# Attention with squared relu and a mixture of adapters: a written order table, and a last batch in two parts with q and k turned by DMA

## The chip, the cores and the metric

The kernel runs on one core of a Trainium2 chip, which has TensorE (PE), VectorE (DVE), ScalarE (ACT), GpSimd (POOL) and SyncE (SP). The metric is the device time of one execution in microseconds (us), taken as the median of a few runs; lower is better. One further execution was taken by the hardware profiler.

## The reference

Eight batches of twelve heads, 448 positions, 64 channels a head. The attention has no softmax: the scores are cut at zero and squared. Its output rows then go through a mixture of eight rank-16 adapters, of which each row uses two.

```python
scores = scale * np.matmul(q, k.transpose(0, 1, 3, 2))          # 8 x 12 x 448 x 448
attn = np.maximum(scores, 0.0) ** 2 / S
x = np.matmul(attn, v)                                          # -> (3584, 768)
logits = x @ w_gate
topk = np.argpartition(-logits, K, axis=1)[:, :K]               # K = 2 of 8
w = np.exp(sel) / (np.exp(sel).sum() + 1e-09)                   # over the two
out = x + sum(w[e] * ((x @ A[e]) @ B[e]) for e in topk)
```

## The kernel before

*Tiling.* A batch is worked on in three quads of four heads; a quad is held as two groups of 64 partitions and two slots. For each of the 24 pairs of batch and quad POOL loads q, k and v (L306), casting them to bf16. PE transposes q and k, 56 small transposes each (L430, `tp`), and DVE copies the result out of PSUM as qT (L444; L452 for the first ones). Then, for each of seven key tiles of 64 keys, PE forms the scores of the quad against all 448 queries (L571, `qk`; four 64x64 matmuls), ACT or DVE applies the scaled relu from PSUM into bf16 (L591 or L593; 128x896 elements), and DVE squares two or three such results at once (L609, `sq`). PE multiplies by v and sums over the seven key tiles in PSUM (L635, `pv`), and ACT or DVE copies the finished 448 columns to xt (L664), which holds the attention output transposed, in bf16. There are 168 key tiles (`n` from 0 to 167).

*The adapters.* The 3584 output rows make 28 tiles of 128, numbered 0 to 27; tile t needs columns 128t to 128t+127 of xt, so tiles 24 to 27 need the last batch, whose columns are 3136 to 3583. Tiles are taken in groups of three, at the end of two, one and one (`gl`). PE multiplies a tile by A and the gate weights at once (L681, six matmuls); the gate chain on DVE with one sigmoid on ACT (L702 to L725) picks two experts and scales; PE transposes the result (L742, `zt`) and it is copied to zT (L751). Each tile's output is made in two halves of 384 columns. PE brings x back by three identity matmuls (L796) and adds the fp32 product with B (L801), 20 PE instructions for a whole tile, and ACT or DVE copies the half out (L836). For tiles 15 to 23 SP has turned x by DMA instead (L767, `xb`, six transposes of 128x384 for a group), and DVE adds it to the product (L831). SP stores a tile from one of four output buffers (`osb`) in two transfers (L852); tiles 24 and 26 are stored by ACT, and tile 27 half by SP and half by ACT.

*The order of the work.* `build` makes a list of operations with their dependencies, ranks and durations. `schedule` is a planner: it plays the list through with a model of engines, PSUM banks and buffers, and each free engine takes the ready operation of lowest rank. The two tables `RANKS` and `ENGINES` nudge single operations. The program is emitted in the order of its start times, each engine running its part in order. PSUM banks and, where an operation can run on ACT or DVE, the engine come from the planner too. The code has a path for turning q and k by DMA (`turn_qk`, `qk_turned`), used from batch `bx` on; with `bx=8` no batch takes it. On that path SP turns q once and k twice, the second time shifted by 64 columns, after DVE has copied k's first 64 columns behind its end (`dup`). The queries then stand in the order 1, 3, 5, 0, 2, 4, 6 of blocks of 64.

The scores go from a pool of four buffers (`a1`, from relu to square) to one of seven (`a2`, from square to the product with v), and the first product of a quad also waits for a square six key tiles ahead (`late`).

Of the kernel before, what the change touches and what calls it, by code (L numbers as in the profile page):

```python
# [14 lines left out]
J = 7  # L15
# [10 lines left out]
STORES = {24: "ACT", 26: "ACT"}  # L26
# [3 lines left out]
PARTS = {b: ((0, S),) for b in range(NB)}  # L30

def parts(*cuts):
    x = [0, *cuts, S]
    return tuple(zip(x, x[1:]))


C = dict(
    tp_=2.3287, qk_=-3.679, sq_=3.7975, pv_=3.3372, xt_=-1.2131, gate_=-0.65203, id_=-0.78412,  # L40
    out_=-0.80943, zt_=6.6019, a12=(4, 7), late=6, merge_x=0, id2=2.6063, ocap=3, tboth=1, sqs=(2, 2, 3), xback=(15, 23), xblat=1.4, xbdur=1.35, bx=8, xlag=6, xh=2, apart=3, gl=(2, 1), tqk=-25.0, tqlat=2.0,
    slack=-0.19633, switch=5.8334, third=4.0894, dve_relu=0.28627, relu_until=400, qk=-2.3217, sq=10,
    pv=1.0506, xt=8.4423, tp=-9.2867, tpe=4.3867, gate_mm=-4.8593, gate=-1.4524, zt=0.2432, zte=2.902,
    id=15.183, out=3.032, pace=6.5353,
)
POOLS = dict(qT=5, a1=C["a12"][0], a2=C["a12"][1], zp=2, zT=3, osb=4, w=3, q=5, k=5, v=8, xb=3)

RANKS = {  # L50
    0: 5, 84: 115, 85: 162, 86: 87, 132: 10, 141: 53, 148: -11, 150: 39, 155: -32, 156: -8, 157: 13, 158:
    -9, 160: -12, 163: -20, 166: -25, 170: -15, 179: -51, 185: -11, 191: -5, 192: 35, 200: 50, 210: 36,
    214: 47, 216: 67, 219: -52, 221: -10, 224: -18, 229: -25, 230: -23, 234: 23, 237: 31, 256: 58, 257:
    61, 276: 60, 290: -45, 292: 8, 310: -28, 314: 54, 318: 3, 321: 23, 332: 49, 342: 72, 350: 58, 355:
    -35, 360: -83, 363: 29, 374: -15, 375: -17, 377: -7, 379: 29, 394: 4, 409: -1, 424: 24, 427: 74, 446:
    -9, 451: -35, 456: 7, 459: 102, 463: -61, 471: -10, 490: 4, 500: -12, 503: -13, 511: 52, 517: 30,
    519: -28, 531: -4, 542: 6, 543: 16, 550: 63, 558: 45, 562: 70, 564: 80, 567: -7, 572: -39, 574: -59,
# [5 lines left out]
    1065: -149,  # L63
}
ENGINES = {
    140: "ACT", 178: "ACT", 233: "ACT", 265: "ACT", 286: "ACT", 298: "ACT", 568: "ACT", 634: "DVE", 852:
    "ACT", 866: "ACT", 881: "ACT",
}

# [16 lines left out]
class Op:  # L86
    def __init__(self, engs, dur, fn, deps=(), after=None, mode=None, kind="", take=(), give=(),
# [12 lines left out]
        for d in self.deps + [after] * (after is not None):  # L100
            d.users.append(self)


class Dma:


    def __init__(self):
# [926 lines left out]
```

## Time and profile before

| what | us |
|---|---|
| median of 3 runs (182.50 to 183.17) | 183.02 |
| span of the profiled execution | 181.7 |
| first relu on ACT starts | 6.7 |
| last relu on ACT ends | 160.2 |
| last PE matmul ends | 176.8 |
| last copy out of PSUM ends | 177.4 |

Durations that matter, from the table of groups (mean of one; neighbours on ACT, and a little on DVE, overlap, so that in a row they cost less):

| line, engine | what | count | mean ns |
|---|---|---|---|
| L591 ACT | relu 128x896 | 155 | 961 |
| L593 DVE | relu 128x896 | 13 | 1088 |
| L609 DVE | square 128x1792 / 128x2688 | 48 / 24 | 1085 / 1550 |
| L444 DVE | qT copy 128x1792 | 21 | 1084 |
| L664 ACT / DVE | xt copy 128x448 | 28 / 20 | 576 / 618 |
| L836 ACT / DVE | osb copy 128x384 | 25 / 13 | 532 / 556 |
| L831 DVE | osb addition 128x384 | 18 | 550 |
| L571, L635 PE | scores, product with v, 64x448 | 672 each | 367, 350 |
| L801 PE | fp32 product with B, two records each | 112 | 515 |

The shares of the page give busy time over the span. A busy PE is not a PE at its peak: matmuls are pipelined, and the records of neighbours overlap. In the chain of waits, where matmuls follow each other, four of 64x448 take 0.19 us and 56 transposes 0.48 us.

### The profile page before, as it was taken

The page shows a single profiled execution, that of the slowest core. Times are in us where ns is not written, and L with a number is a line of the kernel's source. Part 1 is how long each engine was busy: PE and PEld are TensorE (multiplying, and loading weights), DVE is VectorE, ACT ScalarE, POOL GpSimd, SP SyncE. Part 2 cuts the span into 40 slices and gives each one's busy share as a digit, 9 for nine tenths or more (in the row PEclk, how much of TensorE's full clock was granted, in tenths as well). Part 3 has the DMA queues.
Part 4 walks back from the last instruction along what each step waited for, and adds up shares of the span by engine and source line. Part 5 has one row for each costly group of instructions (what it writes and reads, how often), then busy time and mean ns, then how long its engine had stood idle before and what let it go on. Part 6 is the DMA issues. An engine that isn't in the chain of part 4 may idle for free.

```text
span 181.7 us, 7410 instructions
## 1 busy us (share of the span) xinstructions
PE 164.6 (91%) x3198; PEld 96.1 (53%) x3198; DVE 164.7 (91%) x257; ACT 155.5 (86%) x229; POOL 89.8 (49%) x155
## 2 busy tenths in 40 slices
PE   7868698897999998999999999999999999999990
PEld 2433266574465565554755556565654456446640
DVE  1589999999999997999999999999999999998860
ACT  3679999999999997999999999999999999951200
POOL 7999968898786678924975769200000000000000
PEclk9978999999999999999999999999999999999996
DMA  5999999999999999994999999993538264457676
GB/s 92 119 166 151 170 230 136 166 170 185 174 184 186 203 222 194 190 233 108 201 190 257 246 214 199 223 143 78 110 73 203 49 150 112 116 138 208 174 195 156
DMA packets 34450, 30.49 MB, mean 168 GB/s; under 512 B 11952, under 2 KB 30896, under 8 KB 34416
## 3 DMA queue, kind: packets, MB, share of 16 engines
q0 software_dynamic: 22000, 17.03, 64.3%
q1 hardware_dynamic: 11792, 11.90, 24.8%
q10 hardware_dynamic: 624, 1.08, 2.3%
q8 instruction: 25, 0.41, 0.9%
q14 instruction: 9, 0.07, 0.2%
HBM read 33.84 MB, written 11.01 MB: 247 GB/s over the span
## 4 chain that ended last, share of the span: by engine, by line
PE 58%; ACT 17%; DVE 14%; issue 4%; DMA 2%; POOL 2%; ACTq 0%; DVEq 0%; POOLq 0%
PE ps L801 19%; PE ps L571 14%; ACT a L591 14%; PE ps L635 11%; DVE a L609 7%; PE ps L681 4%; PE ps L796 4%; PE ps L430 3%; DMA k<-in_k_dram 2%; DVE qT L444 2%; ACT xt L664 2%; PE ps L382 2%; DVE xt L664 2%; POOL q L306 1%; DVE a L593 1%
## 5 line engine op out<-in xcount | busy, mean ns | idle before, releaser
L591 ACT ACTIVATE a<-ps 128x896 bf16<-128x896 f32 x155 | 133.9, 961 | 2.8 <-PE ps L571 2.5
L609 DVE TENSOR_TENSOR a<-a 128x1792 bf16<-128x1792 bf16 (+1 forms) x72 | 88.5, 1240 | 1.4 <-ACT a L591 1.3
L571 PE MATMUL ps<-qT 64*64 64x448 bf16 x672 | 58.6, 367 | 6.6 <-ACT a L591 4.3
L801 PE MATMUL ps<-B,zT 128*128 128x384 f32 x112 | 47.5, 515 | 0.0
L635 PE MATMUL ps<-a,v 64*64 64x448 bf16 x672 | 43.0, 350 | 1.7 <-ACT a L591 1.6
L571 PEld LDWEIGHTS <-qT 64*64 64x64 bf16 x672 | 22.5, 105 | 35.1 <-issue 27.5
L306 POOL DMA_DIRECT2D q<-in_q_dram x48 | 29.3, 629 | 13.4 <-PE ps L571 6.0
L306 POOL DMA_DIRECT2D v<-in_v_dram x48 | 29.2, 630 | 7.9 <-DMA k<-in_k_dram 4.4
L306 POOL DMA_DIRECT2D k<-in_k_dram x46 | 28.1, 632 | 4.0 <-PE ps L571 2.1
L635 PEld LDWEIGHTS <-v 64*64 64x64 bf16 x672 | 21.7, 106 | 12.0 <-issue 4.8
L444 DVE COPY qT<-ps 128x1792 bf16<-128x1792 bf16 x21 | 22.8, 1084 | 0.2
L801 PEld LDWEIGHTS ps<-B,zT 128*128 128x128 f32 x112 | 17.4, 191 | 4.5 <-DVE osb L831 0.9
L664 ACT CAST xt<-ps 128x448 bf16<-128x448 f32 x28 | 15.2, 576 | 3.6 <-PE ps L635 3.6
L593 DVE TENSOR_SCALAR a<-ps 128x896 bf16<-128x896 f32 x13 | 14.1, 1088 | 0.5 <-PE ps L571 0.4
L681 PE MATMUL ps<-awg,xt 128*128 128x136 bf16 x168 | 12.8, 223 | 1.0 <-issue 0.9
L836 ACT COPY osb<-ps 128x384 f32<-128x384 f32 x25 | 12.8, 532 | 0.6 <-PE ps L801 0.2
L681 PEld LDWEIGHTS <-xt 128*128 128x128 bf16 x168 | 10.4, 98 | 5.5 <-issue 5.0
L796 PE MATMUL ps<-identb,xt 128*128 128x128 bf16 x114 | 12.7, 220 | 0.2
L796 PEld LDWEIGHTS <-xt 128*128 128x128 bf16 x114 | 7.8, 97 | 9.7 <-issue 8.1
L664 DVE CAST xt<-ps 128x448 bf16<-128x448 f32 x20 | 12.2, 618 | 0.7 <-PE ps L635 0.5
L430 PEld LDWEIGHTS <-q 64*64 64x64 bf16 x672 | 10.3, 110 | 4.1 <-DMA q<-in_q_dram 1.2
L430 PE MATMUL ps<-identb,q 64*64 64x64 bf16 x672 | 10.5, 195 | 0.7 <-DMA q<-in_q_dram 0.3
(47 smaller groups left out, 99.0 us busy)
## 6 DMA issues: line engine op xcount, KB each, us to landing
out_dram<-osb SPq DMA_DIRECT2D x50, 192.0 KB, 3.9
q<-in_q_dram POOLq DMA_DIRECT2D x48, 112.0 KB, 4.8
v<-in_v_dram POOLq DMA_DIRECT2D x48, 112.0 KB, 5.1
k<-in_k_dram POOLq DMA_DIRECT2D x46, 112.0 KB, 4.9
out_dram<-osb ACTq DMA_DIRECT2D x4, 192.0 KB, 2.6
B<-in_moe_B_dram POOLq DMA_DIRECT2D x1, 384.0 KB, 6.9
xb<-xt SPq DMA_TRANSPOSE x18, 2.7
a_raw<-in_moe_A_dram POOLq DMA_DIRECT2D x1, 192.0 KB, 6.5
```

Source lines behind the costliest of these rows:

```text
L306: nc.gpsimd.dma_start(out=t[g * PH : g * PH + PH], in_=k.qkv[w][b, g, :, 2 * q : 2 * q + 2, :])
L430: nc.tensor.transpose(k.ps_b[sl * PH : sl * PH + PH, o.banks[g], (w * J + j) * PH : (w * J + j) * PH + PH], source(w, j)[r, sl], k.identb[ ...
L444: nc.vector.tensor_copy(t.rearrange("p g w x -> p g (w x)"), k.ps_b[:, m.banks[0] : m.banks[0] + 2, : 2 * S])
L571: nc.tensor.matmul(out=bank(o, sl)[g * PH : g * PH + PH, at : at + w], lhsT=t[r, g, 1, j * PH : j * PH + PH], rhs=t[r, g, 0, x0:x1], start ...
L591: nc.scalar.activation(out, flat(qk_ops[n], w), ACTF.Relu, scale=k.relu_scale)
L593: nc.vector.tensor_scalar(out, flat(qk_ops[n], w), k.relu_scale, 0.0, op0=ALU.mult, op1=ALU.max)
L609: nc.vector.tensor_mul(a2, T["a1", g0], T["a1", g0])
L635: nc.tensor.matmul(out=bank(head, g)[sl * PH : sl * PH + PH, :w], lhsT=vn[r, sl, j * PH : j * PH + PH], rhs=T["a2", g0][r, i, sl * w : sl ...
L664: evac(w, lambda cp, g=g: cp(k.xt[:, g * QUADS + q, b * S + x0 : b * S + x1], bank(src, g)[:, :w]), deps=[pv_ops[n]], free=[(src, g)], ran ...
L681: nc.tensor.matmul(out=bank(zops[0])[:, t * ZW : t * ZW + ZW], lhsT=k.xt[:, do, 128 * tiles[t] : 128 * tiles[t] + 128], rhs=k.awg[:, do, : ...
L796: nc.tensor.matmul(out=out(h)[:, x * 128 : x * 128 + 128], lhsT=k.xt[:, 3 * h + x, c0 : c0 + 128], rhs=k.identb, start=(x == 0), stop=Fals ...
L801: nc.tensor.matmul(out=out(h)[:, :W], lhsT=T["zT", g0][:, zi], rhs=k.B[:, h * W : h * W + W], start=xb is not None, stop=True, skip_group_ ...
```

## The change

The planner, its ranks and its costs are gone. `ORDER` is a table of words, one for each operation, in the order in which the program is emitted. A word names the operation (`f4` and the like: loads and small things of the start), behind `@` its PSUM bank, behind `:` the engine, A for ACT and D for DVE. `ordered` puts the list of `build` into this order.

The last batch takes the path with q and k turned by DMA (`bx=7`), and its queries are done in two parts: first 320 for all three quads, one key tile at a time, then the other 128, with the scores of four and then three key tiles in one pair of PSUM banks and one relu of 1024 or 768 elements. The key tiles are then 174 numbers, 147 to 167 for the first part and 168 to 173 for the second. The last groups of tiles have three and one (`gl`). There is one pool `a` of eleven buffers; the square is written in place, and the wait on a square six tiles ahead is gone. Other new arguments (`xi`, `om`, `z64`) are off.

In the table `qt63` to `qt71` are the nine DMA transposes of q and k, `xb` those of x, `st` the stores, `b` an output half of PE and `o` its copy (number 2t or 2t+1 for tile t), `z`, `zt` and the `g` words the gate chain.

```diff
-PARTS = {b: ((0, S),) for b in range(NB)}
+PARTS = {b: ((0, S, 1),) for b in range(NB)}
+PARTS.update({7: ((0, 320, 1), (320, 448, 4))})
...
-    out_=-0.80943, zt_=6.6019, a12=(4, 7), late=6, merge_x=0, id2=2.6063, ocap=3, tboth=1, sqs=(2, 2, 3), xback=(15, 23), xblat=1.4, xbdur=1.35, bx=8, xlag=6, xh=2, apart=3, gl=(2, 1), tqk=-25.0, tqlat=2.0,
+C = dict(late=6, xi=(), om=(), merge_x=0, sqs=(2, 2, 3), xback=(15, 23), xblat=1.4, xbdur=1.35, bx=7, xlag=6, xh=2, apart=3, gl=(3, 1), tqlat=2.0)
+GROUP = 2688
...
-POOLS = dict(qT=5, a1=C["a12"][0], a2=C["a12"][1], zp=2, zT=3, osb=4, w=3, q=5, k=5, v=8, xb=3)
+POOLS = dict(qT=5, a=11, zp=2, zT=3, osb=4, w=3, q=5, k=5, v=8, xb=3)
...
+ORDER = """
+f4 f3 f0 f1 f6 f2 f5 f11 f7 f8 f9 f10 f84@0 f85@2 f12 f88 f90 f89 f13 qk0@4 qk1@6 relu0:D qk2@0 relu1:A f14
+f87@2 f91 tp2@4 relu2:A qk3@6 te2 f15 qk4@2 relu3:A relu4:D qk5@0 tp3 relu5:A f17 qk6@6 te3 relu6:A sq0 qk7@2
+qk8@0 qk9@4 relu7:A tp4@6 f16 relu8:D relu9:A qk10@2 te4 qk11@0 relu10:A qk12@4 relu11:D tp5 f18 relu12:A qk13@2
...
+gt12 pv105@2 relu122:D pv106 gsg12 pv107 o21:A qk123@4 pv108 f79 pv109 relu123:A gw12 st20 pv110 gzp12 pv111
+qk124@0 x223:D qk125@6 relu124:A pv112@4 pv113 relu125:D qt65 zt12@3 zt13 zt14 x222:A pv114 qk126@0 zT12:A sq121
+pv115 pv116 relu126:A pv117 f72 qk127@6 pv118 qk128@2 sq123 relu127:A xb90 b24@0 relu128:A b28@1 x236:D xb93
+o24:A sq119 x237:A qk129@6 tp38@2 f75 tp39 relu129:A qk130@4 xb91 te38 b25@0 relu130:A o28:D qk131@6 o25:A
+tp40@2 xb94 tp41 relu131:A sq128 qk132@4 pv119@0 f82 pv120 pv121 relu132:A te40 qk133@6 st24 pv122 pv123
+relu133:A pv124 f78 qk134@4 sq130 qk135@2 pv125 relu134:A qt68 b26@6 x250:A b29@7 dup23 x251:D relu135:A xb92
+sq126 o26:A qk136@4 qk137@0 qk138@2 relu136:A z15@6 o29:D z16 relu137:D relu138:A st28 f81 qk139@4 z17 relu139:A
+sq135 qk140@2 pv126@0 pv127 xb95 relu140:A pv128 qk141@4 gmax15 pv129 sq133 pv130 relu141:A pv131 qk142@2 pv132
+qt69 b27@7 relu142:A gd15 gu15 x265:D gt15 x264:A sq137 pv133@4 qt70 qk143@2 o27:A pv134 qk144@0 gsg15 pv135
+relu143:A z18@7 gw15 z19 xb108 relu144:A gzp15 qk145@2 sq142 z20 relu145:A zt15@6 zt16 zt17 xb111 qk146@0 gmax18
+pv136 zT15:A sq140 pv137 qk147@2 relu146:A b34@6 xb109 gu18 relu147:A gd18 gt18 pv138 o34 pv139 gsg18 qk148@0
+qk149@2 sq144 x279:A b32@6 xb112 relu148:A b30@5 relu149:A o32 x278:A qt71 qk150@0 qk151@2 gw18 relu150:A gzp18
...
+gt21 sq170 gsg21 b39@0 relu172:A st40 z25 gw21 relu173:A b37@6 gzp21 o39 zt21@1 xb131 z26 sq172 zt22 zt23
+pv168@2 zT21:A pv169 pv170@4 gmax24 st38 pv171 x338:A x339:A pv172@0 gd24 gu24 pv173 x343:A gt24 b44@2 x342:D
+x346:A o37 gsg24 x347:A b45@3 gw24 st36 gzp24 z27@6 o44 zt24@7 b42@5 o45 gmax27 b43@4 st44 gd27 gu27 gt27 o42
+gsg27 zt25 b46@0 gw27 gzp27 o43 zt26 zt27@1 b47@5 o46 zT27:A st42 zT24:A b54@6 o47 b55@4 o54:D st46 b52@7 o55:D
+b53@5 st55 st54 o52:D b50@6 o53:D b51@4 st53 o50:D b48@7 o51:D b49@5 st50 o48:A o49:A st49
+"""
...
+def ordered(ops):
+
+    by = {"%s%d" % o.key: o for o in ops}
+    out, done = [], set()
+    for word in ORDER.split():
+        word, _, b = word.partition("@")
+        name, _, e = word.partition(":")
+        o = by.pop(name)
+        o.eng = next(x for x in o.engs if x.startswith(e))
+        if o.want:
+            o.banks = [int(b) + i for i in range(o.want[1])]
+        assert all(d in done for d in o.deps + [o.after] * (o.after is not None)), name
+        done.add(o)
+        out.append(o)
+    assert not by
+    return out
...
+    def turned_span(n):
+        b, u, q, js = order[n]
+        c0, c1 = (x // PH for x in PARTS[b][u][:2])
+        odd = (min(c0, 3), min(c1, 3))
+        even = (max(c0, 3) - 3, max(c1, 3) - 3)
+        return odd, even
+
     def qk_turned(n):
...
+            for y, j in enumerate(js):
+                for r, sl, at, i0, i1 in ((0, 0, 512 - W + y * w, *even), (1, 1, y * w, even[0] + 3, even[1] + 3),
+                                          (0, 1, 512 - no, odd[0] + 4, odd[1] + 4), (1, 0, ne, *odd)):
...
     def relu(n):
         w = width(n)
-        g0, m, i = pair_of[n]
+        g0, m, i, x, total = pair_of[n]
 
         def fn():
             if i == 0:
-                new("a1", ("a1", g0), [128, m, 2 * w], BF16)
-            out = T["a1", g0][:, i]
+                new("a", ("a", g0), [128, total], BF16)
+            out = T["a", g0][:, x : x + 2 * w]
...
-            a2 = new("a2", ("a2", g0), [128, m, 2 * w], BF16)
-            nc.vector.tensor_mul(a2, T["a1", g0], T["a1", g0])
+            a = T["a", g0]
+            nc.vector.tensor_mul(a, a, a)
...
-        if j == 0:
-            wait.append(sq_ops[min(n + c["late"], NS - 1)])
...
-    for o in schedule(build(h)):
+    for o in ordered(build(h)):
         o.fn()
```

## The prediction

> **What bounds the kernel now.** I read the page's busy shares first, then the busy time by stage, then the waits, then the end of the chain of waits, and last the queue of SP, to which the change adds work.
>
> ```profile
> PE 164.6 (91%) x3198; PEld 96.1 (53%) x3198; DVE 164.7 (91%) x257; ACT 155.5 (86%) x229; POOL 89.8 (49%) x155
> ...
> 6.70:20.00 13.30, 10.08 (x277) 4.96 (x263) 11.58 (x14) 12.35 (x15) 12.97 (x21) 0.87 1.11 154
> 20.00:40.00 20.00, 16.71 (x481) 11.53 (x481) 20.00 (x21) 19.95 (x28) 16.72 (x30) 1.00 1.19 175
> ...
> 140.00:160.20 20.20, 19.99 (x336) 10.64 (x329) 19.79 (x32) 19.94 (x29) 0.00 (x0) 1.00 0.51 118
> 160.20:165.00 4.80, 4.76 (x40) 2.43 (x39) 4.47 (x8) 1.21 (x3) 0.00 (x0) 1.00 0.42 109
> 165.00:177.40 12.40, 11.76 (x76) 7.30 (x76) 9.97 (x33) 1.69 (x6) 0.00 (x0) 1.00 0.76 200
> 177.40:181.70 4.30, 0.00 (x0) 0.00 (x0) 0.00 (x0) 0.00 (x0) 0.00 (x0) 0.67 0.58 152
> ```
>
> No single engine stands out in the shares. The stages (columns: length; then PE, PEld, DVE, ACT, POOL) tell more. From the first relu at 6.7 to the end of the last one at 160.2, ACT leaves 3 us unused, 1.0 of them before 20 us, and DVE 4.8, 1.7 of them before 20 us; from there on they are busy 98.6% and 97.8% of the time. From 160.2 to 177.4 ACT is nearly idle (2.9 us busy in 17.2) and PE runs without a gap. The last 4.3 us are the store.
>
> ```profile
> ACT a L591 <- PE ps L571: 1.1, 2, 0.9
> ...
> DVE a L609 <- ACT a L591: 1.3, 2, 1.0
> ...
> 163.49 1.45 PE ps L635 x28
> ...
> 173.30 0.20 PE ps L796 x3
> 173.50 0.70 PE ps L801 x2
> 174.20 0.17 PE ps L796 x3
> 174.37 0.70 PE ps L801 x2
> ...
> 176.84 0.56 DVE osb L836
> ```
>
> The first two lines are most of what the trace names as waits of ACT and DVE between 20 and 160 us: some 1 us each, so the order there leaves little to win back. The chain's end is a ladder of half tiles, 0.87 us each: 0.17 for three identity matmuls, 0.70 for the fp32 product with B.
>
> ```profile
> L767 SPq DMA_TRANSPOSE xb<-xt x18: 1178/1266/1977, 118.7 to 155.3; - x18
> ...
> DMA to landing us min/median/max: 2.3/2.7/4.4
> ```
>
> SP spends 1.27 us on issuing each 128x384 transpose. In the dense stretch from 118 to 140 us its queue is already mostly transposes.
>
> **What the Trainium skill says.** "Perfetto Trace Analysis", Optimization Strategy, says that where the bound changes over time, interleaving the regimes pays beside work within one. That is this trace: ACT and DVE to 160.2, PE after it. "DMA: Bandwidth & Descriptors", DMA Transpose (X-bar), says that the plain DMA transpose takes 2-byte data and is issued from SP or ACT only; here all 18 are SP's, and the nine new ones join the same queue. "VectorE: DVE Perf Modes", The perf-mode tier table, puts a bf16 tensor_tensor from SBUF at two elements per cycle and no more; the squares agree (1.00 us for 1792, 1.47 for 2688 in the chain, 0.52 ns an element), so writing them in place changes no duration.
>
> **The change, part by part.** Prices are what an operation costs in the chain where it stands back to back, since the mean durations include overlap: relu of 896 on ACT 0.81 us ("ACT a L591 x4" takes 3.25), an xt copy 0.43 on ACT and 0.54 on DVE, a relu on DVE 1.02, a qT copy 1.00.
>
> *q and k of the last batch turned by DMA.* Gone are 3x112 transposes on PE: 56 take 0.48 us, so 2.9 us, and three qT copies on DVE, 3.0 us. Added are three copies of 128x64 on DVE; the smallest DVE rows are 0.15 us, so 0.4. PE takes more and narrower matmuls: per key tile 12 in place of 4 for the scores and 10 in place of 4 for the product with v, over the same 448 columns. That is 14x21 = 294 extra starts. Bounds: nothing, if they stream, and 8.6 ns each (the pace of the 64-column transposes), 2.5 us. I take 1.0. PE: -1.9 us; DVE: -2.6.
>
> *320 and 128 queries, four key tiles per relu.* ACT and DVE do 21 relus of 640, three of 1024 and three of 768 for 21 of 896. The slope from 0.81 us at 896 with 1.2 elements per ns gives 0.60, 0.92 and 0.70: relus 0.5 us dearer in all. The squares come to 0.2 more and six extra xt copies to 1. So the split eats about half of what DVE saves. What it buys is time of readiness: tiles 24 to 26 lie wholly in the 320 queries (columns to 3455), so their gate matmuls begin before the last 128 queries are done; only tile 27 is left. The groups at the end are 3 and 1 in place of 2, 1 and 1, one small gate chain less on DVE (0.5).
>
> *The order table.* It decides where everything stands. I counted, in program order, what each engine has ahead of the last relu. ACT before: 155 relus (125.9), 25 xt copies at 0.44 (11.0), 25 osb copies at 0.40 (10.0), 4 zT (1.8), 8 sigmoids at 0.15 (1.2) and one qT half (0.5): 150.3 us. ACT after: 130 + 19 + 3 + 3 relus (121.9), 29 + 6 xt copies (14.8), 24 osb copies (9.6), 6 zT (2.6), and the same 1.7: 150.6. DVE up to the last square, as differences: 4 relus of 896 and 2 of 640 more (+5.5), squares +0.2, k copies +0.4, 2 additions of turned x more (+0.9), against qT -3.0, 6 xt copies (-3.2) and 2 zT (-0.9) that go to ACT: -0.1. So the relu stage holds as much work as ever: what the DMA saves is spent on the narrower pieces and on two more output halves done early (41 for 39). On PE it adds 1.8 us with its changes between 64- and 128-row matmuls, which number 109 before and 111 after. The table also gives DVE 4 of the first 12 relus, in the stage that left DVE 1.7 us idle; up to relu 42 ACT has 1.6 us less ahead of it, DVE the same. Against it: POOL issues the second q before the identity matrix and the rest of k. Two issues of 0.62 us put the identity at 4.4 us in place of 3.1 and the first transposes some 0.3 us later; k_rest lands 1.3 us later, where its relu then starts near 8.9 us. The loads that let relu 7 go (k at 10.6 us) hold the same place in either list, so I take 0 for the start, with 0.5 either way. Idle time won back: 0.5 of the 3 us that ACT has.
>
> *The tail.* PE's work behind the last relu, before: 7 key tiles of P.V at 0.19 (1.3), 9 halves with turned x at 0.70 (6.3), 8 halves at 0.87 (7.0), 4 gate tiles at 0.36 (1.4), 7 transposes at 0.11 (0.8): 16.8, and the trace has 16.6 (160.2 to 176.8). After: 21 key tiles of 128 columns at 0.055 (1.2), 7 halves at 0.70 (4.9), 8 at 0.87 (7.0), 2 gate tiles (0.7), 7 transposes (0.8): 14.6. That is 2.2 us less. The last square (1.0) and its handing over lie beside one half and four products with v; the gate chain of tile 27 (from 166.94 to 168.47 in the trace, 1.5 us, plus two turned additions queued ahead of it on DVE, 1.0) lies beside three halves, 2.1 us. So 0.3 us of it may show.
>
> *The end.* The last tile is stored whole by ACT, two issues as before, but of 192 KB each for 96. ACT's full stores land in 2.6 us and its half ones in 2.5: +0.2.
>
> *Edits with one answer.* One pool of 11 buffers for the scores in place of 4 and 7, squares in place, and a dropped wait of the first product on a square six tiles ahead: nothing, since neither PE nor DVE shows a wait on these.
>
> Sum: relu stage +0.1 (the mean of ACT's +0.3 and DVE's -0.1), idle won back -0.5, tail -2.2, its gate +0.3, end +0.2, and +0.2 for new small waits in a table fixed beforehand: -1.9. Against the profiled span of 181.7 that is 179.8; the runs have a median of 183.02, 1.3 above the span, so about 181.1.
>
> **Rivals.** *Only PE's sum counts.* If PE, 99% busy from 120 us on, is the true bound there, then moving its work from tail to relu stage gains nothing, and only the net -1.9 counts, less the 0.3 of two more changes, the gate and the end: about -1, and with 294 starts at their upper price +0.5. Time 182.0 to 183.5. For it: PE's shares. Against: its matmul records average 360 ns where the chain's pace is 187, so they hide waiting, and ACT has no gaps.
>
> *The table is better packed than I can see.* If the start and the relu stage lose most of their idle time (3 us on ACT, 4.8 on DVE), 2 us more go: 179. For it: the 1.6 us that ACT has less by relu 42. Against: the gaps after 20 us are already down to 2 us of ACT in 140.
>
> *SP falls behind, and it is slower.* The new transposes are 128x896. No trace here shows that size: the issue costs 1.27 us at least, and 2.95 if it grows with the 7 blocks for 3. From relu 126 to 150 the table has five of them in SP's queue, with ten of xb (12.7 us) and four store issues (2.3). That makes 21.4 us at the lower price and 29.8 at the upper one, in a stretch of 24 relus at 0.93 us, 22 us. It decides from about 1.6 us each. Behind them wait the stores of tiles 12 and 14, so the four output buffers, so the evacuations, so PSUM and PE. The scores themselves are covered: the last transpose stands 11 relus (9 us) ahead of its use. Eight us late, less the room of about 4 that the buffers leave, costs up to +4, and with the tail's gain +2: 185. At my middle value, 2.1 us, SP is 3.5 us late and the buffers hide it.
>
> **How the numbers follow.** Forecast 0.50 (180.0 to 182.1), better packed 0.16 (178 to 180), PE's sum 0.16 (182.0 to 183.5), SP 0.18 (184 to 186). A measurement of this kernel can tell about 0.5% (0.9 us) from no change. Faster: all of the first two, so 0.66, and a little of the third, less some of the first that stays above 182.1: 0.66. Same: 0.14. Slower: 0.20, with the table's unknown stalls in it. The range takes in the first and third and half of each other: 178.9 to 184.3; the forecast's own is 180.0 to 182.1.
>
> **What would show it.** Right: the last relu ends at 159.5 to 160.8 in the new profile, PE ends 14.4 to 15.2 us after it, the end from PE's last matmul stays at 4.9 to 5.2, L430 of PE falls by 2.9 us, and SP's issues of the wide transposes take near 2 us. Wrong: a last relu beyond 162 with waits of ACT on the scores (PE or SP), osb evacuations waiting on stores between 125 and 155 us, or a PE gap ahead of tile 27's transpose of over 1 us.

## The result, and the profile after

| | before | after |
|---|---|---|
| median, same runs (lowest to highest) | 183.09 us (182.50 to 183.95) | 194.17 us (193.52 to 195.28) |
| span of the profiled execution | 181.7 | 192.5 |
| last relu ends | 160.2 | 171.5 |
| last PE matmul ends | 176.8 | 186.8 |

The kernel became slower: ratio 1.059, 95% interval 1.054 to 1.065. The forecast was 181.1 us. Here and below, executions over 1.5% above the fastest of the same kernel are left out of the ratios, though not of the medians; the profiled executions of e4, e5, e8, e10 and e18 were of that kind, and from their traces only places and lengths of gaps and the names of waits are read. In the profiled spans the difference is 10.8 us: 11.3 up to the last relu, 1.3 less between it and the last matmul, 0.8 more from there to the end.

The page of the kernel after, shares and three of the rows of 40 slices (4.8 us each):

```profile
PE 168.5 (88%) x3324; PEld 99.9 (52%) x3324; DVE 161.3 (84%) x251; ACT 156.4 (81%) x243; POOL 89.9 (47%) x155
...
PE   7777888898999999996999999961999999999880
...
PEclk9999999999999999999999999997599999999998
DMA  5999999999999599999997999999999467937884
```

ACT and DVE are busy for as long as before (156.4 and 161.3 us against 155.5 and 164.7), but in a longer span. There is a hole in PE, and behind it a stretch of low granted clock, while the DMA row shows nines. The stages of the kernel after, and then of the kernel before (columns: length; PE, PEld, DVE, ACT, POOL; PE's granted clock, 1.00 being full speed; DMA share; GB/s; the share is the time of the packets over the time of 16 engines, and where packets overlap it exceeds 1):

```profile
120.00:130.00 10.00, 8.26 (x199) 4.62 (x198) 9.41 (x11) 8.46 (x13) 4.87 (x9) 1.00 1.29 195
130.00:140.00 10.00, 5.96 (x40) 2.77 (x40) 2.36 (x4) 3.56 (x5) 1.77 (x3) 0.66 1.45 133
140.00:149.00 9.00, 9.00 (x145) 5.54 (x144) 8.50 (x19) 8.59 (x14) 0.00 (x0) 1.00 1.42 200
149.00:171.50 22.50, 22.41 (x476) 14.54 (x465) 21.60 (x41) 21.24 (x38) 0.00 (x0) 1.00 0.65 132
171.50:192.50 21.00, 14.09 (x155) 8.56 (x154) 10.16 (x30) 3.53 (x12) 0.00 (x0) 0.96 0.69 198
```

```profile
120.00:130.00 10.00, 9.88 (x227) 6.04 (x217) 9.80 (x11) 10.00 (x16) 0.00 (x0) 1.00 0.60 97
130.00:140.50 10.50, 10.34 (x139) 5.62 (x140) 10.35 (x26) 10.39 (x18) 0.00 (x0) 1.00 0.56 127
140.50:160.20 19.70, 19.49 (x324) 10.35 (x317) 19.29 (x31) 19.44 (x28) 0.00 (x0) 1.00 0.50 116
160.20:181.70 21.50, 16.52 (x115) 9.73 (x113) 14.45 (x40) 2.90 (x9) 0.00 (x0) 0.93 0.65 170
```

Two things are to be seen. From 120 us on the kernel before has few transfers (share 0.60) and POOL has nothing to do; the kernel after still loads there (POOL 4.87 us) and its DMA engines are full until 149. And ACT, which in the kernel before had next to no idle time there, lies idle 8.4 of the 29 us from 120 to 149. The chain of waits and the list of waits of the kernel after name the place:

```profile
127.46 0.19 PE ps L449 x4
127.65 0.57 PE ps L516 x12
128.22 0.21 PE ps L449 x2
128.43 5.61 issue
134.04 0.58 PE ps L449 x2
```

```profile
PE ps L449 <- issue: 7.2, 2, 5.6
ACT a L468 <- PE ps L449: 12.1, 8, 5.9
```

PE stops after two of the four matmuls of one key tile's scores. It is hardly data that they wait for, since the four read the same tile; the trace has no releaser for it ("issue"). ACT's relus wait for the scores.

How much work had been done by when is seen by counting the relus that had started (counted from 1; windows of half a microsecond, so that each time is up to half a us too late; us):

| relu | before | after |
|---|---|---|
| 100 | 97.0 | 96.5 |
| 120 | 115.5 | 115.5 |
| 126 | 121.0 | 120.0 |
| 130 | 124.0 | 125.5 |
| 140 | 133.5 | 142.5 |
| 147 (the last ahead of the last batch) | 140.5 | 149.0 |

From relu 100 to 126 the order table is within 1 us of the kernel before. Within the next 21 relus it loses some 9 us.

### The profile page after: what moved, and what is told of

It is laid out like the page before. It is cut to its first block, busy times and chain, and to the rows that moved or that the text cites. A ratio compares the mean times of both kernels' runs of the same rounds, so it can differ in the third digit from the quotient of the medians.

```text
span 192.5 us, 7681 instructions
## 1 busy us (share of the span) xinstructions
PE 168.5 (88%) x3324; PEld 99.9 (52%) x3324; DVE 161.3 (84%) x251; ACT 156.4 (81%) x243; POOL 89.9 (47%) x155
## 3 DMA queue, kind: packets, MB, share of 16 engines
q1 hardware_dynamic: 20144, 13.97, 37.2%
## 4 chain that ended last, share of the span: by engine, by line
PE 48%; ACT 18%; DVE 13%; issue 8%; DMA 7%; POOL 4%; DVEq 0%; ACTq 0%; POOLq 0%
PE ps L714 16%; ACT a L468 15%; PE ps L449 9%; PE ps L516 8%; DVE a L485 6%; PE ps L560 3%; DMA v<-in_v_dram 3%; PE ps L705 3%; DVE qT L324 3%; PE ps L423 2%; PE ps L310 2%; ACT xt L544 2%; DMA k_rest<-in_k_dram 2%; DMA q<-in_q_dram 2%; PE ps L509 2%
## 5 line engine op out<-in xcount | busy, mean ns | idle before, releaser
L468 ACT ACTIVATE a<-ps 128x896 bf16<-128x896 f32 (+3 forms) x155 | 131.0, 946 | 12.5 <-PE ps L449 12.1
L485 DVE TENSOR_TENSOR a<-a 128x1792 bf16<-128x1792 bf16 (+3 forms) x75 | 88.1, 1194 | 0.0
L449 PE MATMUL ps<-qT 64*64 64x448 bf16 x588 | 52.6, 377 | 12.3 <-issue 7.2
L516 PE MATMUL ps<-a,v 64*64 64x448 bf16 (+1 forms) x672 | 43.0, 340 | 1.0 <-ACT a L468 0.5
L324 DVE COPY qT<-ps 128x1792 bf16<-128x1792 bf16 x18 | 19.5, 1086 | 3.0 <-PE ps L310 2.9
L470 DVE TENSOR_SCALAR a<-ps 128x896 bf16<-128x896 f32 (+1 forms) x19 | 20.1, 1058 | 1.5 <-PE ps L449 1.4
L544 ACT CAST xt<-ps 128x448 bf16<-128x448 f32 (+2 forms) x40 | 19.6, 537 | 0.1
L560 PEld LDWEIGHTS <-xt 128*128 128x128 bf16 x168 | 10.8, 98 | 6.6 <-issue 5.3
L705 PEld LDWEIGHTS <-xt 128*128 128x128 bf16 x114 | 8.1, 99 | 11.3 <-issue 9.7
L544 DVE CAST xt<-ps 128x448 bf16<-128x448 f32 (+1 forms) x14 | 8.3, 594 | 6.8 <-PE ps L516 6.7
L734 DVE TENSOR_TENSOR osb<-ps,xb 128x384 f32<-128x384 f32 x18 | 9.8, 552 | 2.4 <-PE ps L714 2.0
L310 PEld LDWEIGHTS <-q 64*64 64x64 bf16 x588 | 8.9, 113 | 4.1 <-issue 2.4
```

The lines of the kernel that those rows point to most:

```text
L324: nc.vector.tensor_copy(t.rearrange("p g w x -> p g (w x)"), k.ps_b[:, m.banks[0] : m.banks[0] + 2, : 2 * S])
L449: nc.tensor.matmul(out=bank(o, sl)[g * PH : g * PH + PH, at : at + w], lhsT=t[r, g, 1, j * PH : j * PH + PH], rhs=t[r, g, 0, x0:x1], start ...
L468: nc.scalar.activation(out, flat(qk_ops[n], w), ACTF.Relu, scale=k.relu_scale)
L470: nc.vector.tensor_scalar(out, flat(qk_ops[n], w), k.relu_scale, 0.0, op0=ALU.mult, op1=ALU.max)
L485: nc.vector.tensor_mul(a, a, a)
L516: nc.tensor.matmul(out=bank(head, g)[sl * PH : sl * PH + PH, :w], lhsT=vn[r, sl, j * PH : j * PH + PH], rhs=T["a", g0][r, x + sl * width(n ...
```

## The experiments

18 kernels were run, each on one chip with runs of the kernel before.

| run | what | median us | ratio to before, 95% |
|---|---|---|---|
| e1 | after, last batch's q and k turned on PE | 193.09 | 1.035 to 1.055 |
| e2 | after, 7 buffers for k | 194.56 | 1.043 to 1.063 |
| e3 | after, plain copies for the nine turns | 188.98 | 1.008 to 1.038 |
| e4 | after, 24 more matmuls at the start | 195.66 | not given (2 runs) |
| e5, e8 | after, loads earlier (two orders) | 193.52, 192.02 | 1.032 to 1.058, 1.038 to 1.051 |
| e6, e9 | loads earlier, turned on PE (two places) | 188.42, 188.54 | 1.020 to 1.036, 1.023 to 1.036 |
| e7 | e5, ten key tiles' scores twice | 192.81 | 1.032 to 1.051 |
| e10 | e9, six more turns | 191.79 | 1.038 to 1.050 |
| e11, e13 | before, turning alone (in threes, singly) | 190.53, 191.00 | 1.032 to 1.043, 1.032 to 1.046 |
| e12 | before, six idle turns among its loads | 192.65 | 1.044 to 1.057 |
| e14 | after, loads earlier, turns behind them | 190.12 | 1.029 to 1.040 |
| e16 | e14, late stores on POOL | 186.53 | 1.006 to 1.017 |
| e17 | e16, turns later still | 188.29 | 1.015 to 1.030 |
| e15 | e13, late stores on POOL | 190.89 | 1.026 to 1.042 |
| e18 | e15, turns earlier | 186.06 | 1.004 to 1.011 |

### What stops PE

The page lists a queue of kind "instruction" for each kernel: `q8 instruction: 26, 0.43 MB` here. PE has 3324 matmuls and 3324 weight loads, 6648 records, and 26 times 256 is 6656. So I read q8 as PE's own program, which comes by DMA in blocks of 256 instructions, 128 matmuls with their weights. The count alone proves little (e1 has 6732 such records and also 26 packets); the gaps below do. In "Trainium Architecture — The Big Picture", The software stack, the Trainium skill says that the instruction streams are moved by DMA when a program is loaded; in this trace that can hold only for their beginning, since the packets come during the execution, from 11 to 182 us. The same view cut to 110 to 130 us, first of the kernel after and then of the kernel before:

```profile
q8 instruction: 1, 0.02, 0.4%
...
v<-in_v_dram POOLq DMA_DIRECT2D x13, 112.0 KB, 9.9
...
qT<-k SPq DMA_TRANSPOSE x3, 11.7
xb<-xt SPq DMA_TRANSPOSE x3, 12.6
```

```profile
q8 instruction: 4, 0.07, 1.4%
...
v<-in_v_dram POOLq DMA_DIRECT2D x6, 112.0 KB, 5.4
...
xb<-xt SPq DMA_TRANSPOSE x6, 2.9
```

One block in 20 us in place of four; and these transfers land late (last column: median us from issue to landing): a turn of x in 12.6 us where it took 2.9, a load of v in 9.9 where it took 5.4. The first runs ask whether the turning does this and whether the gap belongs to the program or to the data.

e1 takes the turning away; e2 gives k two more buffers; e3 copies where the change turns (same bytes, larger packets; the last batch's scores are then formed from unturned data); e4 shifts PE's program against its data.

```diff
e1  -C = dict(..., bx=7, ...)          # no qt, no dup
    +C = dict(..., bx=8, ...)          # tp42 to te46 behind relus 141, 145, 153
e2  -q=5, k=5, v=8
    +q=5, k=7, v=8
e3  -nc.sync.dma_start_transpose(out=T["qT", b, q][:, x], in_=t[:, at : at + 2 * S])
    +nc.sync.dma_start(out=T["qT", b, q][:, x], in_=t[:, at : at + 2 * S].rearrange("p (c y) -> p c y", y=128))
e4  -nc.tensor.matmul(k.ps[:, 7, :], lhsT=k.zeros[:, :128], rhs=k.zeros, start=True, stop=True)
    +for y in range(0, 512, 128):      # 32 matmuls for 8
    +    nc.tensor.matmul(k.ps[:, 7, y : y + 128], ...)
```

> The changed kernel with the last batch's q and k transposed by PE again (the six transposes and three qT copies stand in the table where a pair of PSUM banks is free; the nine DMA transposes and three k copies are gone; the 320 and 128 queries and all else as in the changed kernel). Fetch theory (the nine wide DMA transposes, put beside late loads, fill the DMA engines, so that PE's own instruction blocks arrive late and PE runs dry near 128 us): the stall of 5.6 us and the half-clock stretch behind it go, 8 to 9 us, and PE takes some 2 us and DVE 3 us of work back: 184 to 187. Table theory (the written order packs worse in itself, the transposes matter little): 192 or more.

> The changed kernel with seven buffers for k in place of five, since the last batch's first two k stay in theirs from 80 us until they are turned for the second time (room made by laying the first raw k into a part of xt that is written last). Loads then needn't wait for a buffer and should end near 120 us in place of 136. If the stall needs late loads and transposes at the same time, it shrinks to 2 us or less and the time falls to 186 to 189. If the transposes alone do it, the stall stays at 4 us or more and the time at 192 to 195.

> The changed kernel with the nine DMA transposes of q and k as plain copies of the same bytes into the same buffers, at the same places in SP's queue: the last batch's scores are then formed from unturned data. If it is the transposing (many packets under 512 bytes at a low rate) that fills the DMA engines, the stall goes and the time is 184 to 187. If the bytes or the place in SP's queue did it, 192 to 195 stays.

> The changed kernel with the eight warming matmuls of 512 columns at the start cut into 32 of 128 columns: 24 matmuls and 24 weight loads more on PE in the same streaming time. In the changed kernel PE stalls after 1758 and after 2526 matmul records, and the kernel before after 1375; all three are 94 or 95 beyond a multiple of 128. Fetch theory: the stalls again come at 94 or 95 beyond a multiple of 128, so 24 matmuls earlier in the work than now, and the time stays within 2 us of 194. If PE waited there for data, the stall comes at the same place of the work, so at 1782 and 2550 records.

Counting PE's matmul records up to the gap gives the same number in every kernel of this family:

| kernel | gap, us | starts at us | matmuls before it |
|---|---|---|---|
| after | 5.61 | 128.43 | 2526 |
| e1 | 2.54 | 127.46 | 2526 |
| e2 | 4.30 | 131.28 | 2526 |
| e3 | 4.26 | 126.92 | 2526 |
| e4 | 4.19 | 128.17 | 2526 |

In e4 the 24 extra matmuls shift the program against the work, and the gap stays at record 2526, which there falls among transposes; its list of waits:

```profile
PE ps L312 <- issue: 5.1, 2, 4.2
```

So the gap is tied to the program and not to the data. In after, an earlier gap of 1.58 us lies at record 1758, 768 or six blocks before. The packets of q8 themselves settle it. In after q8 moves nothing from 128.4 to 130.2 us, while PE already stands; then, from 130.2 to 132.5, it moves one packet:

```profile
q8 instruction: 1, 0.02, 6.0%
```

That packet of 16384 bytes takes 2.2 us, and PE goes on 1.6 us after its end. In all the runs with a gap at this record (2527 in the kernels made from before), PE's next matmul starts 1.3 to 1.7 us after the end of such a packet. No trace shows when the packet was asked for.

What fills the DMA engines is not the turning alone: with it gone (e1) the gap halves and the time hardly falls, which missed my 184 to 187 us. Nor is it the k buffers alone: e2 issues its last load at 123.6 us, 11 us earlier than after, and keeps a gap of 4.3 us and its time. In e3 the same bytes copied take 13088 packets in the queue of SP for 20144, and these packets 30.4% of the engines' span for 37.2; the kernel is 5 us faster, in two runs. But the stall stays, against what I had written: it is 1.3 us shorter, as in e2, where the turns are all there. The granted clock behind it is 0.83 from 130 to 140 us for 0.66, which is 1.7 us of full clock. The two make up 3 of the 4.3 us between the profiled spans. So the small packets load the engines more; that they lengthen the gap is not shown.

e12 is the reverse test, in the kernel before. It adds six turns that nobody needs, and changes no instruction of PE, ACT or DVE.

```diff
     for o in schedule(build(h)):
         o.fn()
+        n += o.kind == "relu"
+        if o.kind == "relu" and n in (98, 101, 104, 107, 110, 113):
+            nc.sync.dma_start_transpose(out=spare..., in_=h.xt[:, 0, : 128 * DO])
```

> The kernel before with six turns by DMA of 128x768 bf16 added (SBUF to SBUF, into places that nobody reads later), one behind each of relus 98, 101, 104, 107, 110 and 113, so among its last loads; SP waits 24 us for outputs in 90 to 120 us and has room for them. PE, ACT and DVE have the same instructions in the same order. If turns among loads hold back PE's program: a gap of PE of 1.5 us or more that ends in issue at the end of a block, in 105 to 125 us, and 186 to 190 us. If they delay only what waits for a load or a store: gaps that end in a DMA of q, k, v or an output, 184 to 187 us. If neither: within 0.7 us of the kernel before.

192.65 us, 8.5 more than the kernel before. From the chain of waits of e12:

```profile
114.42 0.97 issue
...
122.26 1.79 issue
...
130.71 2.55 issue
```

The three gaps lie at matmul records 2271, 2399 and 2527: exactly 128 apart, one for each block. The trace of before has no such gap there; its own one, 0.91 us at record 1375, lies nine blocks before 2527. The gaps grow from block to block, and the added turns themselves land late, after 12.2 to 16.9 us. Here nothing but DMA work was added, and PE's blocks came late by it.

e10 tried the same on e9. It was 3.3 us slower than e9, but not in the way that I had written: behind 100 us no gap above 0.8 us ended in issue, and PE waited for an output copy whose buffer was still being stored. What such turns delay is whatever is due then.

> e9 with six more turns by DMA of 128x768 bf16 from SBUF to SBUF into places that nobody reads later, three behind relu 114 and three behind relu 121, nothing else changed; PE's instructions are those of e9, one for one. If full DMA engines at 110 to 126 us hold back the block of PE's program: a stall that ends in issue of 2.5 us or more at matmul record 2526, lower granted clock behind it, and e9 plus 3 to 7 us. If the DMA engines have nothing to do with it: no such stall and e9 plus 0 to 1.5 us, the latter from stores that SP issues later.

A gap can cost more than its length. In "TensorE: Matmul & The Clock Gate", What's actually happening, the skill says that an idle window of about 3.4 us brings PE down to half its clock, and that the window runs freely. The traces agree in part: with 5.61 us of gap the granted clock is 0.66 from 130 to 140 us, with 2.54 us (e1) and 2.45 us (e14) 0.83 in the same ten, with 2.45 us again (e16) 1.00 from 126 to 140. So gaps shorter than the window can be enough, and the same gap can go either way; there the measurement decides. As an estimate from these figures, the gap in after and the clock behind it, 10 us at 0.66 or 3.4 us of full clock, come to 9.0 us, about what is lost between relus 126 and 147.

### Loads, turns, or the table

Why are the DMA engines full so late? To turn the last batch's q and k early, the table loads two of its three q and k tiles at relus 70 to 86, and puts the v tiles of batches 5 to 7 behind relus 111 to 139, 15 to 48 relus behind the last reader of the buffers that they take. The planner of before had issued its last load at 114.9 us; the table issues it at 134.8.

e5 and e8 move loads of v and q up and keep the turns where they are; e6 and e9 take the turning away as well, with loads as in the kernel before.

```diff
e5  v5.0 v5.1 v5.2 v6.0 v6.1 v6.2 v7.0 v7.1 v7.2: from relus 111 to 139 to relus 88 to 125; q6.2, q7.2 to 105, 110
e8  like e5 from relu 82 on; q5.2 and q5.1 at relus 84 and 90, some k tiles 2 relus earlier
e6  -bx=7
    +bx=8                              # all loads from batch 4 on as in the kernel before
e9  e6; tp42, tp44, tp46 3 to 6 words later
e7  -for g in range(2 if m else 0):    # on e5
    +for g in [0, 1] * (1 + (b == 7 and n % 2 == 0 and len(js) == 1)) if m else []:
```

> Only the order of eleven loads on POOL is changed: the v tiles of batches 5 to 7 and two q tiles are issued 2 to 27 relus earlier, as soon as their buffers come free, so that the loads end near 120 us with one v tile behind instead of 135 us; the turning by DMA stays. Theory 1 (the block of PE's program at matmul record 2526 comes late because late loads, the turns of x and the turns of q and k share the DMA engines): the stall at record 2526 falls from 5.6 us to under 1.5 us, the granted clock stays near 1.00 in 128 to 140 us, and the time falls to 185 to 189 us; what is left over the kernel before is the last batch (+3.4 us) and the end (+1.0 us) less 1.5 us of tail. Theory 2 (the small packets of the turned q and k are enough by themselves): the stall stays at 4 to 6 us and the time at 192 to 195 us.

> The last batch's q and k turned by PE as before and all loads from batch 4 on issued at the relus at which the kernel before issued them; the order table, the two parts of the last batch, the scores of four key tiles per relu and the new order of the start stay. Theory 1: no stall above 1.5 us at record 2526 and 184 to 188 us, of which 3 us are the turns that are back on PE. Theory 2 for the first run without turning, that the table itself loses the time wherever the DMA engines stand: 190 us or more, with the loss spread over 100 to 160 us and no gap that ends in issue.

> e5 with the order of the loads mended: in e5 PE stood 3.7 us for a q tile of batch 5, whose load had been put behind the v tiles that were moved ahead. Here two q tiles of batch 5 and the k tiles go ahead of those v tiles, and the loads still end near 120 us but for one v tile; the turning by DMA stays. Late loads as the cause: the stall at matmul record 2526 under 1.5 us, no wait for q above 1 us, 186 to 189 us. The small packets of the turned q and k as the cause: a stall of 3 us or more at that record, 190 to 195 us.

> e6 (loads as early as in the kernel before, no turning by DMA) with the three groups of transposes of the last batch set 3 to 6 instructions later each, behind the relu whose PSUM banks they take. In e6 the relus 135 to 147 took 14 us where the kernel before took 11, with PE waiting 1.7 us in three pieces for such a relu. If that placement cost e6 its time: 185 to 187.5 us, so that nearly all of what the table loses is loads, turning and this placement. If the table loses it elsewhere: within 0.7 us of e6's 188.4.

Earlier loads alone gave 1 to 2 us and missed what I had written: in e5 they stood in the way of a q tile that PE then waited for (3.2 us in e7, which has e5's loads), and in e5 and e8 a gap of 3.1 us stays at record 2526. In e7 it is 0.5 us, so with these loads it varies between executions. With the turning gone as well the time falls to 188.4; in e6 the gap is 1.5 us, and in e9 it is gone: no wait of PE for issue above 0.4 us at that place. But e9 is no faster than e6, so the place of the transposes, my explanation of e6's rest, falls.

e7 asks whether PE sets the pace of the last batch, where the stage table above shows PE busy 22.41 of 22.50 us:

> e5 with the scores of ten of the 21 key tiles of 320 queries in the last batch computed twice into the same place (same values; about 0.26 us of PE work each by the 5.4 us that the profile shows for these 168 matmuls, 2.6 us in all), nothing else changed. If PE sets the pace of the last batch (the after kernel has PE busy 10.00 of 10 in 160 to 170 us with ACT 8.82 and DVE 9.39): e5 plus 2.0 to 2.7 us. If the relus on ACT and DVE set it, as the forecast's sum took it: e5 plus 0 to 0.7 us.

PE got 1.6 us more work by its busy time (13.3 us in these matmuls, 11.7 in the kernel after). The medians of e5 and e7 can't tell so little apart. The traces can: the stretch with the added matmuls, from the start of relu 148 to that of relu 168, took 14.7 us, and 13.6 both in the kernel after and in e3. ACT and DVE are each idle 0.9 us in it, and 0.25 us in the kernel after. From its trace, the last batch:

```profile
145.00:167.60 22.60, 22.59 (x542) 15.57 (x543) 21.16 (x40) 20.99 (x37) 0.00 (x0) 1.00 0.56 124
```

PE has no pause, and 1.1 of at most 1.6 us come through. That is more than the 0 to 0.7 us of the view that ACT and DVE set the pace, and less than all of it: in this stretch PE sets most of the pace.

### The turning by itself, and SP's queue

e11 and e13 take the kernel before with its own order and turn q and k of its last batch behind its last load: in threes, and one at a time.

```diff
 for o in plan:                        # the planner's order, q and k transposes of batch 7 left out
     ...
+    if o.kind == "relu" and n in AT:
+        out += [dup, turn, turn, turn]      # e11: AT = (122, 130, 138)
+        out += [turn]                       # e13: AT = (125, 128, 131, 134, 136, 139, 142, 145, 148)
```

> The kernel before with its own order of instructions and its own loads, and one thing of the change alone: q and k of the last batch turned by DMA (nine transposes of 128x896 on SP behind relus 122, 130 and 138, when its loads have ended) in place of the 168 transposes on PE and three copies of 1.1 us on DVE; the batch stays in one part. If the turning costs only where it meets loads: no gap of PE that ends in issue above 1.2 us, and 180.5 to 184 us, the gain being at most the three copies and 3 us of PE. If its small packets cost by themselves: a gap of 2 us or more and 186 to 192 us.

> e11 with the nine turns issued one at a time, behind relus 125, 128, 131, 134, 136, 139, 142, 145 and 148, after the last loads and with room for stores between them, nothing else changed. In e11 the relus up to 147 kept the pace of the kernel before (141.0 us against 140.5), and then an output waited 5.7 us for its buffer, whose store stood behind three turns on SP. If only the place of the turns cost e11 its 6 us: 182 to 184.5 us, so within 1 us of the kernel before, with up to 1.6 us to gain from three DVE copies of 1.1 us that are gone. If the turning costs wherever it stands: 187 us or more, with gaps of PE ahead of which the trace shows a DMA of xb or out, or issue.

Both miss the good case. e11 has a gap of 1.5 us at record 2527, so the turns can hold back a block even where the loads are over, and then one long wait. From the waits of e11, and its SP:

```profile
DVE osb L831 <- DMA out_dram<-osb: 5.7, 1, 5.7
```

```profile
141.37 1.22 SPq L522 DMA_TRANSPOSE qT<-q  x1
142.69 2.59 SPq L522 DMA_TRANSPOSE qT<-k  x2
145.33 1.25 SPq L767 DMA_TRANSPOSE xb<-xt  x1
146.67 1.18 SPq L852 DMA_DIRECT2D out_dram<-osb  x2
```

Three turns stand ahead of a store, whose output buffer the next tile waits for. One at a time (e13) the stores pass and relu 155 starts at 149.0 us (before: 148.0), but now the last turn goes out at 154.4 us and PE waits for it:

```profile
PE ps L548 <- DMA qT<-k: 3.5, 1, 3.5
```

After that, relu 165 starts 6.5 us late. So SP's queue seems to have no room for nine turns in that stretch of the kernel before. e15 gives it room, with the stores of tiles 12 to 23 on POOL, and e18 issues the turns closer together:

```diff
e15 +STORES.update({t: "POOL" for t in range(12, 24)})
e18 -AT = (125, 128, 131, 134, 136, 139, 142, 145, 148)
    +AT = (124, 126, 128, 130, 132, 134, 136, 138, 140)
```

> e13 with the stores of tiles 12 to 23 issued by POOL, which has nothing to do after its last load at 115 us, in place of SP; nothing else changed. In 118 to 162 us of e13 SP is issuing nearly without a pause, and the last turn of the third q and k tile went out at 154.39 us. If SP's queue is what the turning lacks: no wait for qT above 0.5 us and 180.5 to 184 us, the lower end if the three copies that DVE no longer makes (3.3 us, half of it on the pace of ACT and DVE together) come through. If it is the DMA engines: 187 us or more, with turns and stores landing later than the 2.3 to 4.3 us of e13.

> e15 with the nine turns behind relus 124, 126, ... 140 (the last 8 relus earlier than in e15), nothing else changed. If one late turn was e15's loss: no wait for qT above 0.5 us and 181.5 to 184.5 us, so no slower than the kernel before. If the turning costs as such: 187 us or more.

e15 still has its last turn at 153.2 us, behind turns of x that wait for their data, and PE waits 4.8 us. e18's trace names no wait for qT any more, and with 186.06 us (183.28 to 189.29; the kernel before 184.07) it is 0.4 to 1.1% slower than before: it recovers most of the loss and shows no gain from the three DVE copies that are gone.

e14, e16 and e17 do the same to the changed kernel, whose table of PE, ACT and DVE stays.

```diff
e14 loads from batch 4 on at the relus of the kernel before
    qt63 ... qt71 behind relus 125 128 131 134 136 139 142 145 148
e16 -STORES = {24: 'ACT', 26: 'ACT'}
    +STORES = {24: 'ACT', 26: 'ACT', **{t: 'POOL' for t in range(12, 24)}}
e17 qt63 ... qt71 behind relus 130 132 134 136 138 140 142 145 148; three v loads behind relus 106, 109, 114
```

> The changed kernel with two things moved: the loads from batch 4 on at the relus at which the kernel before issues them, and the nine turns of q and k one at a time behind the same nine relus as in e13. The order table of PE, ACT and DVE, the two parts of the last batch and the start stay as in the changed kernel. If the place of loads and turns made the loss: 183.5 to 187 us, no gap that ends in issue above 1.2 us, and what is left over the kernel before is the last batch and the end (the changed kernel took 43.5 us from relu 147 on, the kernel before 41.3). If the table loses by its own: 188 us or more.

> e14 with the stores of tiles 12 to 23 issued by POOL in place of SP. If SP's queue made e14's late turns of x (an output waited 3.6 us for xb, another 6.1 us for a store): 183 to 187 us, with e14's stall of 2.5 us at record 2526 left. If not: within 1 us of e14's 190.1.

> e16 with the turns of q and k 3 to 6 relus later (first behind relu 130 in place of 125) and three loads of v 7 to 10 relus earlier (behind relus 106, 109 and 114), so that between 118 and 127 us there is one load, no turn of q or k and the turns of x only. If the block of PE's program came late in e16 because of what lay there: the stall at record 2526 under 1.2 us and 183 to 185.5 us. If the turns of x alone keep it: a stall of 2 us or more and within 0.7 us of e16's 186.5.

e14 gains 4 us and e16 another 3.6: 186.53 us. Of the 11 us, some 7.6 come back by moving DMA issues alone. The waits of PE in e16, and then in e17:

```profile
PE ps L447 <- issue: 2.5, 1, 2.5
```

```profile
PE ps L422 <- DMA qT<-k: 4.3, 1, 4.3
...
PE ps L448 <- issue: 1.1, 1, 1.1
```

In e17 the gap at record 2526 falls to 1.1 us as theory had it, and relu 147 starts at 139.3 us, 2.1 us before e16 (141.4) and 0.8 before the kernel before (140.2). Then the last turn is late, PE waits 4.3 us, the granted clock falls to 0.66, and the kernel ends behind e16. No version ran faster than the kernel before; one with e17's loads and an earlier last turn was not tried.

## Why the prediction was wrong, by its steps

**The transposes: right.** They fall from 20.9 to 18.3 us of PE's busy time, 2.6 for the forecast's 2.9.

**The work ahead of the last relu: right.** The sum had it unchanged, ACT +0.3 and DVE -0.1. From the start to the end of the last relu, before and then after:

```profile
0.00:160.20 160.20, 148.10 (x3084) 86.40 (x3085) 150.28 (x218) 152.60 (x221) 89.80 (x155) 0.99 0.96 167
```

```profile
0.00:171.50 171.50, 154.42 (x3170) 91.32 (x3171) 151.11 (x222) 152.84 (x231) 89.94 (x155) 0.98 1.09 166
```

ACT has 0.24 us more and DVE 0.83. For these two engines the 11.3 us are idle time. (The last batch takes 22.5 us for 19.7, but ACT and DVE together have 4.1 us more work in it, done earlier in the kernel before.)

**The step that failed: "+0.2 for new small waits in a table fixed beforehand".** This term of the sum was the only one that stood for waits; it measured some 9 us, between relus 126 and 147, where PE stood 5.61 us for a late block of its program and then ran at a lower clock. The prediction's own sign came true: a last relu beyond 162 (171.5), with ACT waiting for the scores (12.1 us). I had counted every instruction of PE, ACT and DVE in the table's order, and looked at its DMA issues only as time on SP. I never asked when POOL's loads would be issued: the words for v stand in the table for anyone to count, 15 to 48 relus behind the release of their buffers. And I took the DMA engines as having room because the kernel before has it after 118 us, which it has because its loads are over. No term of the sum stood for what turns and loads do to each other, or to PE's program, on these engines. Neither one alone is the loss: taking the turns away (e1) or moving the loads (e5, e8) gives about 1 to 2 us back, both together (e6, e9) some 5.7, and moving loads, turns and stores (e16) 7.6.

**The slower rival: half right.** "SP falls behind" took 2.1 us for the issue of a wide transpose. In the kernel after it is 1.3 for q and 2.6 for k (medians), 2.2 on average. (By its own prices SP falls behind from 1.4 us on, 22 less 15.0 over five, not from the 1.6 that it names.) Its mechanism, stores and turns behind each other on SP, is what e11 and e13 show, with turns of x in place of stores in e15, and taking stores off SP gave 3.6 us from e14 to e16. But in the kernel after itself only one output copy waits for a store (1.6 us); there the late block of PE's program came first. The rival's 185 us had the sign, not the place.

**The tail: nearly right.** Forecast 14.4 to 15.2 us from the last relu to PE's last matmul; measured 15.3, with PE's gap ahead of tile 27's transposes of 1.2 us, above the 1 us that I had named as wrong. In e16 the last relu ends at 165.6 and PE at 179.6: 14.0 us, 2.6 less than before.

**PE's sum: not rejected as a mechanism.** In e7 most of PE's added work comes through in the last batch, so the reasons that I gave against it, long records and an ACT without gaps, don't rule it out there. Its 182.0 to 183.5 us failed like the forecast, for want of any term for the late block. **The "better packed" table: not shown.** e17 is 0.8 us ahead of the kernel before at relu 147, with some of the work that this one has done by then still to do.

**The end: +0.8 us for +0.2** in the kernel after. In e16 it is 4.8 us, as in the kernel before (4.9). Why it is longer in after was not tested.

**The start: near the forecast,** which was 0 with 0.5 either way: relu 21 starts at 22.2 us for 21.7, relu 42 at 41.9 for 41.1.

**What remains.** e16 is 0.6 to 1.7% above the kernel before. One gap of 2.5 us and a wait of PE of 1.4 us for an output addition are seen. By e16's trace the last relu ends 5.4 us late with the work unchanged, and 2.7 us come back behind it. Whether a table with all issues in place would reach the 179 to 181 us of the sum is open.

## What to carry to other kernels

A hand-made order has to place the loads, turns and stores as carefully as the arithmetic: for each, count how long its buffer has been free, what is in flight at that time, and what stands behind it on its queue. In a program of thousands of instructions the program itself is one more user of the DMA engines; where a gap of PE ends in "issue" in the middle of an operation, count the records up to it in several kernels, and look for a packet of the instruction queue at its end. And whether a PE that is busy all the time is the bound is seen by giving it more work, and by timing the stretch that has the work rather than the whole kernel.

## What the runs showed of the hardware that was not expected

- PE's program comes by DMA while the kernel runs, in packets of 16384 bytes (0.43 MB in 26), each for 128 matmuls and their weight loads by the distance of the gaps in e12, and comes late when the DMA engines are full: gaps of 0.97, 1.79 and 2.55 us at three blocks in a row in e12, 5.61 us in after. PE goes on 1.3 to 1.7 us after the packet's end.
- A turn by DMA from SBUF to SBUF loads the engines more than a copy of the same bytes: the packets of SP's queue take 37.2% of their span in after and 30.4% in e3. Six turns of 128x768 (1.2 MB, by the queue's 13.08 MB against 11.90, of some 32 MB that the kernel moves) cost the kernel before 8.5 us, with 5.3 us of gaps of PE. A turn of 128x384 lands in 2.9 us in the kernel before, in 12.6 in after, where the engines are full.
- A wait of PE of 4.3 us (e17) or 5.6 us (after) goes with a mean granted clock of 0.66 in ten microseconds that hold its end. A gap of 2.45 us was followed by 0.83 in e14 and by 1.00 in e16.
